# Windowed attention on Trainium2: softmax sums of four heads in one matmul, and value matmuls in alternating row tiles

## The chip, the cores and the metric

The kernel runs on one core of a Trainium2 chip. The metric is device time in microseconds (us), the median of several executions. All timed runs quoted here were fast, unless said otherwise. The granted clock, the mean share of full speed that the chip grants the tensor engine, was 0.998 or more in them, but for e11 (0.991 to 0.997) and the single run of e12 (0.993). Ratios are the mean time of one kernel's fast runs over the mean of the fast runs of the kernel before in the same rounds, so they are not quite the ratio of the medians quoted next to them. The kernel before takes about 510 us.

## The reference, cut to what matters

Two attention blocks share an input of 2048 rows of 1024; a gate mixes their outputs. The change touches block B only: each query attends to 8 keys, at distances 0, 2, ..., 14 behind it.

```python
H = 32; Dh = D // H                      # 32 heads of 32
W, dil = 8, 2
logits = einsum("bhsd,bhswd->bhsw", q, kg) * Dh ** -0.5
logits = where(mask, logits, -1e9)
attn = softmax(logits, axis=-1)
o = einsum("bhsw,bhswd->bhsd", attn, vg)
return o.transpose(...).reshape(B, S, D) @ wo
# ... and at the end: g * A(x) + (1 - g) * B(x)
```

The kernel sorts rows by parity, so a query's 8 keys are neighbours. A block of up to 57 queries then needs 64 keys, and a mask takes care of which.

## The kernel before

The program is a list of operations that a scheduler orders for each engine, with an estimated cost for each. Block B's attention is cut into 18 "fills". A fill is two halves (h) of up to 57 queries, for all 32 heads. It has three steps: the scores S on the tensor engine (64 small matmuls), exponential and mask, and then the "value burst": for each head and half one matmul of the values with the exponentials E, and one of a block of ones with E, which gives the softmax sums. ScalarE then takes exp(-ln(sum)) and VectorE multiplies.

```python
def s_fn(e):                                   # scores: 64 matmuls, 32 rows x 64 weight columns
    for c in range(8):
        for h in range(2):
            for j in range(4):
                last = e.matmul(SO[j]...[64 * h:64 * h + 64, :], kT[32 * j:32 * j + 32, ...], qT[...],
                                start=True, stop=True, tile_position=(32 * j, 64 * h))
    return last
P.op("pe", s_fn, 0.45, mode="r", ...)
# ... E = exp(scores), E *= mask
for g in range(2):                             # two groups of 16 heads
    def each(e, g=g):
        for o in range(2):                     # 0: values, 1: sums
            for c in range(4):
                for h in range(2):
                    for j in range(4):
                        hd = 16 * g + 4 * c + j
                        w = vt[64 * h:64 * h + 64, hd * 32:hd * 32 + 32] if o == 0 else ones[64 * h:64 * h + 64, :]
                        last = e.matmul(SO[2 * g + h].ap((4 * o + c) * nq, (4 * o + c + 1) * nq)[32 * j:32 * j + 32, :], w,
                                        E[64 * h:64 * h + 64, (8 * j + 4 * g + c) * nq:(8 * j + 4 * g + c + 1) * nq],
                                        start=True, stop=True, tile_position=(64 * h, 32 * j))
        return last
    P.op("pe", each, 0.35, mode="c", ..., name="PV")
    # ... ScalarE: L = Ln(sums); L = Exp(-L); VectorE: qT = values * L
```

A matmul here is a pair of instructions: a load of its weights (64 rows x 32 columns, into one of 8 tiles of the array: row tile h, column tile j), and the matmul that streams nq = 57 columns (56 in the last fills) through that tile. A value burst is 2 x (32 + 32) = 128 pairs. Between bursts the engine does dense 128x512 matmuls of the projections. I count the pairs of a burst from 0.

## Time and profile before

| | before |
|---|---|
| time | 510.26 us (509.35 to 511.56) |
| tensor engine (PE) busy | 99% of the span, granted clock 0.999 |
| VectorE / ScalarE busy | 52% / 39% |
| small pairs: 18 score bursts, 18 value bursts | 1152 and 2304 |

The page of the kernel before: busy time of each engine with its share and number of instructions, then the chain of work that ended last, by engine and by line. PEld is the weight-load side of the tensor engine, DVE is VectorE, ACT ScalarE, POOL GpSimd, SPq the queue of SyncE that issues transfers; "issue" is time in which the engine waited for nothing that the profile shows.

```profile
PE 501.5 (99%) x6121; PEld 239.4 (47%) x6121; DVE 265.0 (52%) x456; ACT 196.2 (39%) x335; POOL 6.6 (1%) x30
...
PE 96%; SPq 2%; DMA 1%; ACT 1%; issue 0%; DVE 0%
PE ps_all L1324 75%; PE ps_all L1674 11%; PE ps_all L1449 4%; PE ps_all L1427 2%; PE ps_all L1599 1%; SPq L1294 1%; DMA w_4_52<-in_B_wqkv_dram 1%; PE ps_all L1520 1%; PE ps_all L1577 1%; SPq L1299 0%; PE ps_all L1392 0%; ACT ra_50_98 L1601 
```

The tensor engine bounds the kernel, and the value bursts (line 1449) hold 4% of the chain, the scores (line 1427) 2%.

Groups of matmuls by shape, kernel before: line, engine, names, rows*columns of the tile, streamed operand, count, then busy us and mean ns of one.

```profile
L1427 PE MATMUL ps_all<-qT_50,kT_51 32*64 32x57 bf16 x1024 | 11.2, 200 | 0.0
L1449 PE MATMUL ps_all<-E_40_88,ones_58 64*32 64x57 bf16 x512 | 7.3, 195 | 0.0
...
L1449 PE MATMUL ps_all<-E_39_87,v_43_91 64*32 64x57 bf16 x192 | 2.4, 192 | 0.0
```

The 195 ns of one matmul say little: they overlap, and 512 of them take 7.3 us. What counts is the time from start to start. For that, here is one value burst in order of time on the weight-load side, kernel before (start us, length us, what):

```profile
144.38 0.19 PEld L1449 LDWEIGHTS ps_all<-E_40_88,v_44_92 64*32 64x32 bf16 x32 [0.42 <-DVE mx_54_102 L1280]
144.51 0.44 PEld L1449 LDWEIGHTS ps_all<-E_40_88,ones_58 64*32 64x32 bf16 x32
144.87 0.35 PEld L1449 LDWEIGHTS ps_all<-E_40_88,v_44_92 64*32 64x32 bf16 x32
145.16 0.35 PEld L1449 LDWEIGHTS ps_all<-E_40_88,ones_58 64*32 64x32 bf16 x32
145.55 0.55 PEld L1324 LDWEIGHTS ps_all<-xT_49,w_5_53 128*128 128x128 bf16 x4
```

From the first small load to the next dense one are 1.17 us for 128 pairs. (The releaser in brackets is merely the last event before: every burst that follows dense work starts 93 or 94 ns over a normal step in this trace, whatever is named.) The single starts in the trace give the anatomy. Dense matmuls start every 216 ns; the "cost" of a burst below is the time from the last dense matmul before it to the first after it, less those 216 ns:

```
value burst before, 128 pairs, cost 1262 ns (all six that stand alone: 1261 or 1262)
  last dense matmul to first small one     309 ns, so 93 over a normal step
  loads of pairs 0 to 31                   3 to 4 ns apart
  loads of pairs 32 and 33                 25 and 101 ns later; pair 33 is 229 ns after pair 0
  from there                               8 or 9 ns apart (8.33 on average), but one step of 34 ns at pair 96
  (by matmuls, as in the prediction: pair 32, the 33rd, starts 223 ns after pair 0)
  last load to the next dense load         128 ns
score burst, 64 pairs, cost 727 ns: the same quick 32 (loaded in 114 ns, those above in 104) and the same 8.33 ns
```

### The profile page before, as it was taken

Reading aid. Unit: us, or ns where it says so; the run is one execution under the profiler, and the core shown is the slowest. Engines: PE = TensorE matmul, PEld = TensorE weight load, DVE = VectorE, ACT = ScalarE, POOL = GpSimd, SP = SyncE. Lnnn points to the kernel's source line nnn. Section 1 sums busy time; section 2 is a strip of 40 time slices with the busy share of each in tenths; the row PEclk is TensorE's granted clock in tenths of the full one; section 3 lists DMA queues with packets and bytes.
Section 4 is the critical chain, followed back from the end, with each engine's and each line's share of the span. In section 5 each row is a group of like instructions: output and inputs, shape, how many; then the busy total and the mean of one; then the engine's idle time right before and its main releaser. Section 6 shows DMA issues by size and latency. Waiting matters only on the chain.

```text
span 507.9 us, 13377 instructions
## 1 busy us (share of the span) xinstructions
PE 501.5 (99%) x6121; PEld 239.4 (47%) x6121; DVE 265.0 (52%) x456; ACT 196.2 (39%) x335; POOL 6.6 (1%) x30
## 2 busy tenths in 40 slices
PE   8999999999999999999999999999999999999996
PEld 3444444444555555555555555544444444444443
DVE  3112245655667675554555555488776673334443
ACT  1111111111444454655565465479965453110000
POOL 5000000000000000000000000000000000000000
PEclk9999999999999999999999999999999999999999
DMA  8999980000033060100010100500000000002212
GB/s 227 198 209 320 352 248 1 1 0 1 24 104 109 23 199 24 35 25 23 23 35 23 35 3 4 168 0 0 1 1 1 1 1 0 3 29 76 83 74 76
DMA packets 47417, 35.04 MB, mean 69 GB/s; under 512 B 22261, under 2 KB 43125, under 8 KB 47354
## 3 DMA queue, kind: packets, MB, share of 16 engines
q1 hardware_dynamic: 46810, 33.59, 23.2%
q8 instruction: 50, 0.82, 0.7%
q10 hardware_dynamic: 544, 0.52, 0.3%
q14 instruction: 13, 0.11, 0.1%
HBM read 21.51 MB, written 8.40 MB: 59 GB/s over the span
## 4 chain that ended last, share of the span: by engine, by line
PE 96%; SPq 2%; DMA 1%; ACT 1%; issue 0%; DVE 0%
PE ps_all L1324 75%; PE ps_all L1674 11%; PE ps_all L1449 4%; PE ps_all L1427 2%; PE ps_all L1599 1%; SPq L1294 1%; DMA w_4_52<-in_B_wqkv_dram 1%; PE ps_all L1520 1%; PE ps_all L1577 1%; SPq L1299 0%; PE ps_all L1392 0%; ACT ra_50_98 L1601 0%; ACT ra_52_100 L1601 0%; ACT ra_51_99 L1601 0%; ACT e_27_75 L1333 0%
## 5 line engine op out<-in xcount | busy, mean ns | idle before, releaser
L1324 PE MATMUL ps_all<-xT_49,w_6_54 128*128 128x512 bf16 x512 | 118.1, 379 | 0.1
L1324 PE MATMUL ps_all<-w_4_52,xT_49 128*128 128x512 bf16 x512 | 116.0, 379 | 0.7 <-DMA xT_49<-in_A_x_dram 0.7
L1324 PEld LDWEIGHTS ps_all<-xT_49,w_6_54 128*128 128x128 bf16 x512 | 49.5, 98 | 59.2 <-ACT ra_52_100 L1601 0.6
L1324 PEld LDWEIGHTS ps_all<-w_4_52,xT_49 128*128 128x128 bf16 x512 | 48.3, 98 | 59.4 <-DMA xT_49<-in_A_x_dram 2.1
L1324 PE MATMUL ps_all<-w_7_55,xT_49 128*128 128x512 bf16 x256 | 59.3, 379 | 0.0
L1324 PE MATMUL ps_all<-xT_49,w_5_53 128*128 128x512 bf16 x256 | 58.4, 379 | 0.0
L1674 PE MATMUL ps_all<-w_7_55,qT_50 128*128 128x512 bf16 (+1 forms) x264 | 55.4, 373 | 0.0
L1324 PE MATMUL ps_all<-w_5_53,xT_49 128*128 128x512 bf16 x192 | 42.7, 379 | 0.0
L1674 PEld LDWEIGHTS ps_all<-w_7_55,qT_50 128*128 128x128 bf16 x264 | 25.8, 98 | 29.7
L1324 PEld LDWEIGHTS ps_all<-xT_49,w_5_53 128*128 128x128 bf16 x256 | 24.5, 98 | 29.2 <-issue 0.4
L1324 PEld LDWEIGHTS ps_all<-w_7_55,xT_49 128*128 128x128 bf16 x256 | 24.1, 98 | 28.0 <-issue 0.3
L1324 PEld LDWEIGHTS ps_all<-w_5_53,xT_49 128*128 128x128 bf16 x192 | 18.8, 98 | 22.6
L1359 ACT ACTIVATE qT_50<-ps_all 128x512 bf16<-128x512 f32 x15 | 9.0, 597 | 37.1 <-PE ps_all L1324 37.1
L1356 ACT ACTIVATE kT_51<-ps_all 128x512 bf16<-128x512 f32 x14 | 8.4, 597 | 35.5 <-PE ps_all L1324 35.5
L1358 DVE TENSOR_SCALAR xT_49<-ps_all,g_65 128x512 bf16<-128x512 f32 x15 | 11.2, 749 | 19.9 <-PE ps_all L1324 19.9
L1280 DVE TENSOR_TENSOR mx_54_102<-mx_54_102,kT_51 128x1024 bf16<-128x1024 bf16 x16 | 11.1, 691 | 16.9 <-ACT kT_51 L1356 16.9
L1280 DVE TENSOR_TENSOR mx_54_102<-mx_54_102,qT_50 128x1024 bf16<-128x1024 bf16 x16 | 11.1, 691 | 16.8 <-ACT qT_50 L1359 16.7
L1459 DVE TENSOR_TENSOR qT_50<-ps_all,L_41_89 128x456 bf16<-128x456 f32 (+1 forms) x18 | 11.3, 628 | 11.6 <-ACT L_41_89 L1458 11.6
L1355 DVE CAST kT_51<-ps_all 128x512 bf16<-128x512 f32 x18 | 12.3, 684 | 7.6 <-PE ps_all L1324 7.6
L1433 ACT ACTIVATE E_39_87<-ps_all 128x1824 bf16<-128x1824 f32 (+1 forms) x9 | 15.2, 1688 | 2.3 <-PE ps_all L1427 1.8
L1433 ACT ACTIVATE E_40_88<-ps_all 128x1824 bf16<-128x1824 f32 (+1 forms) x9 | 15.2, 1688 | 0.6
L1324 PE MATMUL ps_all<-w_5_53,pq_8_56 128*128 128x512 bf16 x64 | 15.1, 379 | 0.0
(179 smaller groups left out, 518.8 us busy)
## 6 DMA issues: line engine op xcount, KB each, us to landing
w_5_53<-in_B_wqkv_dram SPq DMA_DIRECT2D x2, 1024.0 KB, 7.8
w_6_54<-in_B_wqkv_dram SPq DMA_DIRECT2D x2, 1024.0 KB, 8.5
w_4_52<-in_A_wqkv_dram SPq DMA_DIRECT2D x2, 1024.0 KB, 9.3
w_7_55<-in_A_wqkv_dram SPq DMA_DIRECT2D x2, 1024.0 KB, 8.2
w_5_53<-in_A_wo_dram SPq DMA_DIRECT2D x2, 1024.0 KB, 5.6
w_6_54<-in_A_wqkv_dram SPq DMA_DIRECT2D x2, 1024.0 KB, 5.4
w_7_55<-in_B_wo_dram SPq DMA_DIRECT2D x2, 1024.0 KB, 5.9
out_dram<-o_60_108 SPq DMA_DIRECT2D x8, 256.0 KB, 2.0
```

Source lines behind the costliest of these rows:

```text
L1280: P.op("dve", lambda e, m=m, op=op: e.tensor_tensor(m[:, 0:n], m[:, 0:n], src, op), 0.08 + n / 1920.0, reads=[m.all(), reg], writes=[m.all()],
L1294: return P.op("sp", lambda e: e.dma_start_transpose(xT[:, :, t * 128:(t + 1) * 128], x2[e_, r * 128:(r + 1) * 128, :]), 1.5, writes=[xT.pa ...
L1324: last = e.matmul(bank.ap(), lhs(dc), rhs(dc), start=(dc == 0), stop=(dc == 7))
L1355: fd = lambda e: e.tensor_copy(dst, src())
L1356: fa = lambda e: e.activation(dst, src(), ACT.Copy)
L1358: fd = lambda e: e.tensor_scalar(dst, src(), scale, None, op0=ALU.mult)
L1359: fa = lambda e: e.activation(dst, src(), ACT.Copy, scale=scale)
L1427: last = e.matmul(SO[j].ap(c * nq, (c + 1) * nq)[64 * h:64 * h + 64, :], kT[32 * j:32 * j + 32, c, t0 + k0[h]:t0 + k0[h] + 64], qT[32 * j: ...
L1433: P.op("act", lambda e: e.activation(E[:, 0:32 * nq].rearrange("p (j q) -> p j q", j=4), ps[:, 4:8, 0:8 * nq], ACT.Exp), act(32 * nq), rea ...
L1449: last = e.matmul(SO[2 * g + h].ap((4 * o + c) * nq, (4 * o + c + 1) * nq)[32 * j:32 * j + 32, :], w, E[64 * h:64 * h + 64, (8 * j + 4 * g ...
L1459: P.op("dve", lambda e, L=L, pb=pb, g=g: e.tensor_tensor(qT[:, 4 * g:4 * g + 4, t0 + qs:t0 + qs + 2 * nq].rearrange("p c (h q) -> p h c q" ...
L1674: last = e.matmul(bank.ap(0, f1 - f0), qT[:, dc, t * 128:(t + 1) * 128], ws[3][:, dc, f0:f1], start=(dc == 0), stop=(dc == 7))
```

## The change: intent and diff

The sums of four heads c are neighbours in E, and the weights (ones) are the same, so one matmul of 4 x 57 = 228 columns can do the work of four. Each half of a burst then has 32 + 8 = 40 pairs, a burst 80 instead of 128. The values, besides, alternate between the two row tiles instead of doing four pairs in one and then four in the other. Two cost estimates for the scheduler change.

```diff
-P.op("pe", s_fn, 0.45, mode="r", ...)
+P.op("pe", s_fn, 0.55, mode="r", ...)
 ...
-for o in range(2):
-    for c in range(4):
-        for h in range(2):
-            for j in range(4):
-                ... one matmul of nq columns, weights vt or ones ...
+for c in range(4):
+    for j in range(4):
+        for h in range(2):
+            ... value matmul of nq columns into SO[2 * g + h].ap(c * nq, (c + 1) * nq)[32 * j:32 * j + 32, :] ...
+for j in range(4):
+    for h in range(2):
+        last = e.matmul(SO[2 * g + h].ap(4 * nq, 8 * nq)[32 * j:32 * j + 32, :], ones[64 * h:64 * h + 64, :],
+                        E[64 * h:64 * h + 64, (8 * j + 4 * g) * nq:(8 * j + 4 * g + 4) * nq],
+                        start=True, stop=True, tile_position=(64 * h, 32 * j))
-P.op("pe", each, 0.35, mode="c", ...)
+P.op("pe", each, 0.36, mode="c", ...)
```

More of the change, by code (lines that the diff above doesn't have):

```diff
@@ L1429, in s_fn @@
                 return last
-            P.op("pe", s_fn, 0.45, mode="r", reads=[kT.part((0, 8), (t0 + k0[0], t0 + k0[1] + 64)), qT.part((0, 8), (t0 + qs, t0 + qs + 2 * nq))],
+            P.op("pe", s_fn, 0.55, mode="r", reads=[kT.part((0, 8), (t0 + k0[0], t0 + k0[1] + 64)), qT.part((0, 8), (t0 + qs, t0 + qs + 2 * nq))],
                  writes=[s.iv for s in SO], name="S")
@@ L1442, in each @@
                     def each(e, g=g):
-                        for o in range(2):
-                            for c in range(4):
+                        for c in range(4):
+                            for j in range(4):
                                 for h in range(2):
-                                    for j in range(4):
-                                        hd = 16 * g + 4 * c + j
-                                        w = vt[64 * h:64 * h + 64, hd * 32:hd * 32 + 32] if o == 0 else ones[64 * h:64 * h + 64, :]
-                                        last = e.matmul(SO[2 * g + h].ap((4 * o + c) * nq, (4 * o + c + 1) * nq)[32 * j:32 * j + 32, :], w,
-                                                        E[64 * h:64 * h + 64, (8 * j + 4 * g + c) * nq:(8 * j + 4 * g + c + 1) * nq],
-                                                        start=True, stop=True, tile_position=(64 * h, 32 * j))
+                                    hd = 16 * g + 4 * c + j
+                                    e.matmul(SO[2 * g + h].ap(c * nq, (c + 1) * nq)[32 * j:32 * j + 32, :], vt[64 * h:64 * h + 64, hd * 32:hd * 32 + 32],
+                                             E[64 * h:64 * h + 64, (8 * j + 4 * g + c) * nq:(8 * j + 4 * g + c + 1) * nq],
+                                             start=True, stop=True, tile_position=(64 * h, 32 * j))
[3 more added lines that the diff above has]
+                                                E[64 * h:64 * h + 64, (8 * j + 4 * g) * nq:(8 * j + 4 * g + 4) * nq],
+                                                start=True, stop=True, tile_position=(64 * h, 32 * j))
                         return last
                     bi = [SO[2 * g].iv, SO[2 * g + 1].iv]
-                    P.op("pe", each, 0.35, mode="c", reads=[vt.all(), ones.all(), E.all()], writes=bi, name="PV")
+                    P.op("pe", each, 0.36, mode="c", reads=[vt.all(), ones.all(), E.all()], writes=bi, name="PV")
                     L, _ = Lr.next()
```

## The prediction

> **What bounds the kernel.** The tensor engine. The page's first part: PE 501.5 of 507.9 us (99%), VectorE 52%, ScalarE 39%; the granted clock is full throughout; the chain that ended last is 96% PE. Line 1449 (sums and values) is 4% of it, the scores (line 1427) 2%. PE time saved there is saved from the whole; nothing else can give much.
>
> **What one value burst costs.** There are 18. In order of time, dense 128x512 matmuls start every 216 ns. From the last one before a burst to the first after it are 1478 ns, so a burst costs 1262 ns, the same to 2 ns wherever no other small burst adjoins: 22.7 us in all. Inside, by starts:
> - 93 ns over a normal step before the first small matmul;
> - 32 matmuls 3 to 4 ns apart, then a pause of 97 ns; the 33rd starts 223 ns after the first;
> - then one pair (weight load, matmul) per 8.33 ns, 4.17 ns per instruction; one hiccup of some 26 ns;
> - 128 ns from the last start to the next dense matmul.
>
> Sum: 93 + 223 + 95 x 8.33 + 26 + 128 = 1261.
>
> The score burst (64 pairs, weights of 64 columns, already alternating between row tiles) keeps the same 8.33 ns after the same quick 32. [...]
>
> **What the change does.** Streamed columns stay the same. Per burst, 64 sums of 57 columns become 16 of 228: 80 pairs, not 128. The instruction order built from both kernels shows hardly anything else moved.
> - Removed: 48 x 8.33 = 400 ns.
> - Added: the last sum streams 171 columns more; [...].
> - [...]
> - Alternating row tiles: about 0, as the scores alternate and get the same pace.
>
> Expected burst: 93 + 223 + 47 x 8.33 + (0 to 30) + 199 = 905 to 935 ns, saving about 340. Times 18: 6.1 us, all on the chain. ScalarE and VectorE have slack; the scheduler's new costs shift a few bursts by eight matmuls: about 0.
>
> **Predicted: 504.2 us (-1.2%), 8 in 10 between 502.6 and 506.6.** Chances: faster by over 2% 0.02, within 2% 0.97, slower by over 2% 0.01.
>
> **What would show it right.** Bursts of about 0.92 us between dense matmuls, 8.33 ns steps in the values after the 32nd, about 200 ns from the last sum to the next dense matmul; dense matmuls and score bursts (727 ns) unchanged; PE 98 to 99% busy.
>
> **What would make it wrong.** (a) Two row tiles of the same columns cannot stream long matmuls at once: eight sums then take about 190 ns per half, the burst exceeds 1.0 us, the gain is 3 to 4 us. (b) [...] alternation then speeds up the values, and the gain exceeds 7 us. (c) The pause of 97 ns moves or repeats.

The sum is whole: 93 + 223 + 47 x 8.33 + (0 to 30) + 199 = 905 to 935 ns a burst, about 340 saved, 6.1 us for 18 bursts. The 199 is the 128 ns of the trace and 71 more, for the 171 columns that the last sum streams beyond 57. The 0 to 30 leaves room for the hiccup of 26 ns and for a wait of the next value behind the first half's sums, mostly hidden. At the dense pace of the trace, 512 columns in 216 ns, these times are, as estimates: 72 ns for 171 columns; 96 ns for a sum of 228, and so a wait of 29 beyond eight pairs at 8.33 ns; and 192 ns for two such sums one after the other, the "about 190" of (a).

## The result, and the profile after

The changed kernel took 504.05 us (503.54 to 504.76, 4 runs), the kernel before in the same rounds 509.85 us. The ratio is 0.9881, with a 95% interval of 0.9854 to 0.9909: 1.2% faster, inside the range and within 0.2 us of the number predicted. Run again later, it gave 504.56 us and 0.9880.

The page after, the same parts as before:

```profile
PE 488.5 (97%) x5190; PEld 232.6 (46%) x5257; DVE 264.6 (53%) x456; ACT 192.9 (38%) x335; POOL 6.6 (1%) x30
...
PE 95%; issue 2%; DMA 1%; ACT 1%; SPq 0%; DVE 0%
PE ps_all L1324 76%; PE ps_all L1677 11%; PE ps_all L1427 2%; PE ps_all L1447 2%; PE ps_all L1602 1%; PE ps_all L1452 1%; PE ps_all L1523 1%; DMA xT<-in_A_x_dram 1%; PE ps_all L1580 1%; ACT ra L1604 0%; PE ps_all L1392 0%; SPq L1294 0%; SPq
```

Weight loads fell from 6121 to 5257, by 864 = 18 x 48, as intended. The chain gives 3% to values and sums (lines 1447 and 1452) where it gave 4%. PE busy fell to 97% and "issue" appeared: that is no new idle time. The trace has 67 fewer matmuls than loads, and in the bursts I looked at the missing record is the first dense matmul after the burst; its load is there. The traces of e2 and e3 below, with 128 pairs and the time of the kernel before, also lack 67 records and also read 97%. I therefore measure the ends of bursts by loads.

Groups of matmuls by shape, after (values, sums, scores):

```profile
L1447 PE MATMUL ps_all<-E,v 64*32 64x57 bf16 x1024 | 12.4, 191 | 0.0
L1427 PE MATMUL ps_all<-qT,kT 32*64 32x57 bf16 x1024 | 11.3, 200 | 0.0
L1452 PE MATMUL ps_all<-E,ones 64*32 64x228 bf16 x256 | 10.4, 265 | 0.0
```

The value burst that answers to the one shown of before, weight-load side, after:

```profile
144.14 0.19 PEld L1447 LDWEIGHTS ps_all<-E,v 64*32 64x32 bf16 x32 [0.42 <-DVE mx L1280]
144.27 0.24 PEld L1452 LDWEIGHTS ps_all<-E,ones 64*32 64x32 bf16 x8
144.43 0.37 PEld L1447 LDWEIGHTS ps_all<-E,v 64*32 64x32 bf16 x32
144.75 0.15 PEld L1452 LDWEIGHTS ps_all<-E,ones 64*32 64x32 bf16 x8
145.00 0.98 PEld L1324 LDWEIGHTS ps_all<-xT,w 128*128 128x128 bf16 x6
```

From the first small load to the next dense one are now 0.86 us, 0.31 less. By single starts:

```
value burst after, 80 pairs, cost 960 ns (alone: 959 to 961)
  entry                                    93 over a normal step, as before
  pairs 0 to 31 quick; pair 33             231 ns after pair 0 (before: 229)
  from there                               8.33 ns, with steps of 22 and 21 ns at pairs 65 and 66 and of 34 ns at pair 72
  matmuls 40 and 41                        39 and 17 ns steps, then quick ones that catch up; matmul 40 starts 97 ns after 32,
                                           the sum in the same tile (228 columns: 96 ns at the dense pace, an estimate)
  last load to the next dense load         198 ns (before: 128)
score burst 728 ns
```

Adding up the costs of all small bursts of the trace (the few small matmuls of other parts included) gives 43.08 us before and 37.67 after, 5.41 less. The spans of the two profiled executions are 507.9 and 502.5 us, 5.4 less. So the gain is in the bursts. That the two agree so closely is luck: the span less its small bursts is 464.9 us in both, but 464.3 to 466.4 us over all the traces here without e11 and e12. The medians differ by 5.8 us; the remaining 0.4 us is inside the spread of single runs, which is over 1 us.

### The profile page after: what moved, and what is told of

Same layout as the page of the kernel before. It is cut to its first block, busy times and chain, and to the rows that moved or that the text cites. A ratio compares the mean times of both kernels' runs of the same rounds, so it can differ in the third digit from the quotient of the medians.

```text
span 502.5 us, 11582 instructions
## 1 busy us (share of the span) xinstructions
PE 488.5 (97%) x5190; PEld 232.6 (46%) x5257; DVE 264.6 (53%) x456; ACT 192.9 (38%) x335; POOL 6.6 (1%) x30
## 4 chain that ended last, share of the span: by engine, by line
PE 95%; issue 2%; DMA 1%; ACT 1%; SPq 0%; DVE 0%
PE ps_all L1324 76%; PE ps_all L1677 11%; PE ps_all L1427 2%; PE ps_all L1447 2%; PE ps_all L1602 1%; PE ps_all L1452 1%; PE ps_all L1523 1%; DMA xT<-in_A_x_dram 1%; PE ps_all L1580 1%; ACT ra L1604 0%; PE ps_all L1392 0%; SPq L1294 0%; SPq L1299 0%; ACT e L1333 0%; ACT ra L1605 0%
## 5 line engine op out<-in xcount | busy, mean ns | idle before, releaser
L1324 PE MATMUL ps_all<-w,xT 128*128 128x512 bf16 x922 | 207.8, 379 | 5.6 <-issue 4.0
L1324 PE MATMUL ps_all<-xT,w 128*128 128x512 bf16 x747 | 169.2, 379 | 2.5 <-issue 1.9
L1324 PEld LDWEIGHTS ps_all<-w,xT 128*128 128x128 bf16 x960 | 91.3, 98 | 110.3 <-issue 1.7
L1324 PEld LDWEIGHTS ps_all<-xT,w 128*128 128x128 bf16 x768 | 73.9, 98 | 88.8 <-ACT ra L1604 0.6
L1677 PE MATMUL ps_all<-w,qT 128*128 128x512 bf16 (+1 forms) x259 | 55.2, 373 | 0.3
L1677 PEld LDWEIGHTS ps_all<-w,qT 128*128 128x128 bf16 x264 | 25.8, 98 | 29.7
L1433 ACT ACTIVATE E<-ps_all 128x1824 bf16<-128x1824 f32 (+1 forms) x18 | 30.4, 1687 | 3.1 <-PE ps_all L1427 2.0
L1331 ACT ACTIVATE e<-ps_all 128x512 bf16<-128x512 f32 x32 | 19.1, 597 | 31.6 <-PE ps_all L1324 30.8
L1333 ACT ACTIVATE e<-ps_all 128x512 bf16<-128x512 f32 x32 | 19.2, 601 | 29.3 <-PE ps_all L1324 27.8
L1337 DVE SCALAR_TENSOR_TENSOR pk<-ps_all,e 128x512 bf16<-128x512 f32 x32 | 22.0, 688 | 0.8
L1604 ACT ACTIVATE ra<-ps_all,eps 128x512 f32<-128x512 f32 x32 | 21.5, 688 | 2.2 <-PE ps_all L1602 2.0
```

The lines of the kernel that those rows point to most:

```text
L1324: last = e.matmul(bank.ap(), lhs(dc), rhs(dc), start=(dc == 0), stop=(dc == 7))
L1331: P.op("act", lambda e: e.activation(e_[:, :], bank.ap(), ACT.Exp), act(512), reads=[bank.iv], writes=[e_.all()])
L1333: P.op("act", lambda e: e.activation(e_[:, :], bank.ap(), ACT.Exp, accum_out=qe[:, col:col + 1]), act(512) + 0.1, reads=[bank.iv], writes= ...
L1337: P.op("dve", lambda e: e.scalar_tensor_tensor(out=dst, in0=bank.ap(), scalar=0.0, in1=e_[:, :], op0=ALU.max, op1=ALU.add), dps(512), read ...
L1433: P.op("act", lambda e: e.activation(E[:, 0:32 * nq].rearrange("p (j q) -> p j q", j=4), ps[:, 4:8, 0:8 * nq], ACT.Exp), act(32 * nq), rea ...
L1604: P.op("act", lambda e: e.activation(R[:, :], db.ap(), ACT.Ln, bias=eps[:, :]), act(512), reads=[db.iv, eps.all()], writes=[R.all()])
```

## The experiments

The theory that entered them: a burst's pairs, behind the quick 32 and the pause, come at a fixed 8.33 ns per pair, whatever they stream, so pairs removed are what pays; long sums cost something at the end of the burst. Rivals: the alternation of row tiles pays; the scheduler's new order pays; or streamed columns set the time.

| run | pairs | burst alone, ns | all small bursts, us | median us (before beside it) | ratio (95%) |
|---|---|---|---|---|---|
| before | 128 | 1262 | 43.08 | | |
| the change, run again | 80 | 960 | 37.67 | 504.56 (511.08) | 0.9880 (0.9861 to 0.9899) |
| e1 merge only | 80 | 958 | 37.62 | 504.57 (510.09) | 0.9887 (0.9871 to 0.9903) |
| e2 alternation only | 128 | 1262 | 43.08 | 509.86 (510.09) | 0.9995 (0.9981 to 1.0010) |
| e3 costs only | 128 | 1262 | 43.08 | 509.86 (510.09) | 0.9990 (0.9977 to 1.0003) |
| e4 sums of two heads | 96 | 1018 | 38.69 | 505.17 (510.09) | 0.9899 (0.9883 to 0.9915) |
| e5 sums first | 80 | 934 | 37.21 | 503.61 (509.49) | 0.9883 (0.9867 to 0.9900) |
| e7 short sums (wrong result) | 80 | 861 | 35.89 | 502.65 (509.49) | 0.9861 (0.9843 to 0.9880) |
| e8 pairs put back | 128 | 1267 | 43.27 | 509.78 (509.49) | 1.0004 (0.9987 to 1.0020) |
| e9 sums of eight, first | 72 | 961 | 37.68 | 505.28 (509.49) | 0.9910 (0.9896 to 0.9924) |
| e10 late sums | 80 | 869 | 36.02 | 502.99 (511.08) | 0.9846 (0.9823 to 0.9868) |
| e11 sums of eight, in the middle | 72 | 822 | 40.04 | 513.49 (511.08) | 1.0047 (1.0027 to 1.0067) |
| e12 one signal | 80 | 934 | 41.51 | 514.45 (one run) | |

All runs passed the check of results, e7 too, though its sums are wrong by construction; so that check does not tell right sums from those of e7. No run has the number e6. In e11 and e12 the column of all small bursts holds the waits inside them.

### e1: the merge alone

The change without the alternation and with the old costs.

```diff
-for c in range(4):
-    for j in range(4):
-        for h in range(2):          # values, and the sums likewise
+for c in range(4):
+    for h in range(2):
+        for j in range(4):
```

> The sums of four heads are merged, but the values keep the order of the kernel before (four column tiles of one row tile, then the other), and the scheduler keeps its old costs. Theory ([...] 8.33 ns per pair of weight load and matmul): a value burst of 960 +- 15 ns as with the whole change, total within 0.15% of the whole change, about 0.988 of before. Rival (the alternation of row tiles gives a part of the gain): burst clearly above 975 ns and total above 0.990 of before.

Measured: 958 ns and 0.9887. The merge alone gives the whole gain.

### e2: the alternation alone

The kernel before with `for j` outside `for h`; sums stay at 57 columns.

> Only the order is changed: values and sums alternate between the two row tiles, the sums stay at 57 columns, 128 pairs. Theory: burst 1262 +- 10 ns, ratio to before 1.000 +- 0.002. Rival: burst shorter by 50 ns or more, ratio 0.998 or less.

One value burst of e2, weight-load side:

```profile
145.84 0.19 PEld L1449 LDWEIGHTS ps_all<-E,v 64*32 64x32 bf16 x32 [0.42 <-DVE mx L1280]
145.97 0.44 PEld L1449 LDWEIGHTS ps_all<-E,ones 64*32 64x32 bf16 x32
146.33 0.35 PEld L1449 LDWEIGHTS ps_all<-E,v 64*32 64x32 bf16 x32
146.62 0.35 PEld L1449 LDWEIGHTS ps_all<-E,ones 64*32 64x32 bf16 x32
147.00 0.55 PEld L1324 LDWEIGHTS ps_all<-xT,w 128*128 128x128 bf16 x4
```

The lengths are those of the kernel before, line for line. The burst costs 1262 ns, the ratio is 0.9995. Half of the change, by its title, does nothing. In this kernel four neighbouring pairs of one row tile and alternating ones go at the same 8.33 ns; in neither order do two neighbouring pairs use the same tile. At that pace a load in the kernel before starts 4 ns after the matmul ahead of it, in the same row tile too, where that matmul streams for some 24 ns (an estimate: 57 columns at 512 in 216 ns).

### e3: the scheduler's costs alone

The kernel before with 0.55 and 0.36 as the two costs.

> Only the scheduler's two costs are changed. Theory: the bursts stay at 1262 (values) and 727 ns (scores), only the number of dense matmuls between some bursts changes; ratio 1.000 +- 0.002. Rival (the new order is itself worth time): ratio 0.997 or less.

Measured: bursts of 1262 and 727 ns, ratio 0.9990. The interval allows 0.2%, so a tenth of a per cent from the order is not excluded; the summed bursts of 43.08 us show no part of the 5.4 us in it.

### e4: sums of two heads

The change with 16 sums of 114 columns per half instead of 8 of 228.

```diff
-for j in range(4):
-    for h in range(2):
-        ... ap(4 * nq, 8 * nq) ... E[..., (8 * j + 4 * g) * nq:(8 * j + 4 * g + 4) * nq]
+for d in range(2):
+    for j in range(4):
+        for h in range(2):
+            ... ap((4 + 2 * d) * nq, (6 + 2 * d) * nq) ... E[..., (8 * j + 4 * g + 2 * d) * nq:(8 * j + 4 * g + 2 * d + 2) * nq]
```

> The whole change, but sums of two heads in one matmul of 114 columns: 96 pairs, the same streamed columns. Theory: burst 1050 +- 25 ns (960 + 16 x 8.33 = 1093, less 48 ns because the last sum streams 114 columns fewer), exit from the last sum to the next dense matmul about 151 ns, total about 0.9915 of before. Rival (streamed columns set the burst): no difference from before or from the whole change.

Measured: 1018 ns, below the stated range; the exit was 150 ns as expected (the 48 ns are an estimate, 114 columns at the dense 512 in 216 ns). The steps at pairs 65 and 66 of the whole change are missing here. That is worth 27 ns (22 + 21 instead of 2 x 8.33 = 17, so 26 to 27), and 960 + 133 - 48 - 27 = 1018. So those steps belong to the long sums, and 114 columns are too short to cause them.

### e7: sums that stream only 57 columns

A wrong result: the first head's sum stands for all four.

```diff
-... ap(4 * nq, 8 * nq) ... E[..., (8 * j + 4 * g) * nq:(8 * j + 4 * g + 4) * nq]
+... ap(4 * nq, 5 * nq) ... E[..., (8 * j + 4 * g) * nq:(8 * j + 4 * g + 1) * nq]
-Ln reads the four sums
+Ln reads the one sum, broadcast
```

> Wrong result on purpose: as the whole change, with 16 sums of 57 columns instead of 228 (the sum of the first head stands for all four). 80 pairs, 36 percent of the streamed columns gone. Theory: burst 865 +- 10 ns: exit 128 instead of 198 ns, and the two steps of 22 and 21 ns in the second half's values (pairs 65 and 66) vanish, if they are the echo of the wait behind the long sums. If they stay, 890. Rival (streamed columns set the burst): burst below 750 ns.

```profile
144.12 0.19 PEld L1447 LDWEIGHTS ps_all<-E,v 64*32 64x32 bf16 x32 [0.42 <-DVE mx L1280]
144.24 0.24 PEld L1452 LDWEIGHTS ps_all<-E,ones 64*32 64x32 bf16 x8
144.40 0.35 PEld L1447 LDWEIGHTS ps_all<-E,v 64*32 64x32 bf16 x32
144.70 0.15 PEld L1452 LDWEIGHTS ps_all<-E,ones 64*32 64x32 bf16 x8
144.88 1.19 PEld L1324 LDWEIGHTS ps_all<-xT,w 128*128 128x128 bf16 x7
```

Measured: 861 ns, exit 127, no steps at 65 and 66. Three eighths of the streamed columns are gone (three quarters of the sums, which are half of all; the 36 percent of the expectation is a slip), yet the burst is only 99 ns shorter: 71 at the exit, 27 from the steps. Streamed columns do not set the pace.

### e8: the pairs put back

After each half's sums, 24 repeats of them on 8 columns only, which write the same values again.

```diff
+for _ in range(3):
+    for j in range(4):
+        for h in range(2):
+            last = e.matmul(SO[2 * g + h].ap(4 * nq, 4 * nq + 8)[32 * j:32 * j + 32, :], ones[64 * h:64 * h + 64, :],
+                            E[64 * h:64 * h + 64, (8 * j + 4 * g) * nq:(8 * j + 4 * g) * nq + 8], ...)
```

> The whole change and, after each half's sums, 24 repeated sums of only 8 columns, which write the same values again: 128 pairs as in the kernel before, with few more columns than after. Theory: the gain is given back: burst 1250 to 1290 ns, ratio to before 1.000 +- 0.003. Rival (streaming or weight columns matter): burst within 100 ns of the 960 of the change.

```profile
144.10 0.19 PEld L1447 LDWEIGHTS ps_all<-E,v 64*32 64x32 bf16 x32 [0.42 <-DVE mx L1280]
144.23 0.24 PEld L1452 LDWEIGHTS ps_all<-E,ones 64*32 64x32 bf16 x8
144.39 0.28 PEld L1458 LDWEIGHTS ps_all<-E,ones 64*32 64x32 bf16 x24
144.59 0.37 PEld L1447 LDWEIGHTS ps_all<-E,v 64*32 64x32 bf16 x32
144.91 0.15 PEld L1452 LDWEIGHTS ps_all<-E,ones 64*32 64x32 bf16 x8
144.97 0.28 PEld L1458 LDWEIGHTS ps_all<-E,ones 64*32 64x32 bf16 x24
145.27 1.19 PEld L1324 LDWEIGHTS ps_all<-xT,w 128*128 128x128 bf16 x7
```

Again 1.17 us from the first small load to the next dense one. The burst costs 1267 ns and the ratio is 1.0004: 48 nearly empty pairs per burst give the whole gain back. 960 + 48 x 8.33 - 92 (exit 106 instead of 198) = 1268. This settles the main cause: what is paid for is the pair, not what it streams, apart from the 99 ns that e7 showed the long sums to add.

### e5: sums first

The sums of each half ahead of its values.

> The whole change with the eight long sums of each half issued ahead of its values. Theory: the long stream of the last sum no longer delays the next dense matmul (exit 128 instead of 198 ns), and the wait of the first values for the first sums falls into the pause after the 32nd pair, so the burst is 890 +- 25 ns; total lower than the whole change by about 1.2 us (0.9855 of before). Rival (the exit is a fixed cost of the mode change and the wait moves to the front): burst 950 ns or more.

A miss: 934 ns instead of 890, above the stated range. The exit fell to 127, against 198 in the change, so the exit is no fixed cost, and the steps at 65 and 66 went, as expected (71 + 27 saved). But pair 33 came 301 ns after pair 0 instead of 229: the wait was not hidden in the pause, it pushed the pause back by 72 ns. 960 - 71 - 27 + 72 = 934. In time, 503.61 us and 0.9883 cannot be told from the change itself; the 0.46 us fewer in the bursts are too little for that.

### e9: sums of eight heads, first

One matmul of 456 columns per tile, ahead of all values; sums in two banks, values in the other two; one logarithm, exponential and product per fill.

```diff
+def sums(e):  ... SO[h].ap(0, 8 * nq) ... E[64 * h:64 * h + 64, 8 * j * nq:8 * (j + 1) * nq] ...        # 8 pairs
+def each(e):  ... SO[2 + h].ap(c * nq, (c + 1) * nq) ... for c in range(8) ...                          # 64 pairs
```

> Sums of eight heads in one matmul of 456 columns, ahead of all values, in two banks of their own; the values of all heads in the other two; one logarithm, one exponential and one product per fill instead of two. 72 pairs. Theory: eight sums occupy their tiles 190 ns, then 24 quick values, so the 33rd pair is at about 270 ns instead of 223, partly caught up; burst 93 + 223..270 + 39 x 8.33 + 128 = 770 to 820 ns; with 80 rather than 128 pairs already worth 5.4 us, this is 2.5 to 3.5 us more: total about 0.982 of before. Rival (long streams do not overlap across all eight tiles): burst above 900 ns.

A miss: 961 ns. (Its 190 ns are an estimate: 456 columns at 512 in 216 ns are 192.) Eight pairs fewer, and the burst is no shorter than that of the change. Pair 33 came 396 ns after pair 0. The expectation had named over 900 ns as the sign of its rival, that long streams do not overlap across tiles; the single starts exclude it, since the eight values behind the sums wait 180 ns once and then start 3 or 4 ns apart, so the eight tiles had streamed together. And the total, 505.28 us, is longer than the bursts explain: right after the last fill the tensor engine waits for the transposed key-value product (0.66 us in one place) where it does not in the change, since the scheduler made another order there; steps over 216 ns between dense loads add up to 6.1 us in this trace and 5.1 in that of the change.

The three values of pair 33 fit one pattern. The delay against short values is 301 - 229 = 72 ns for sums of 228 columns and 396 - 229 = 167 ns for 456. From the dense pace (512 columns in 216 ns) the additional streaming is, as an estimate, 171 x 216 / 512 = 72 and 399 x 216 / 512 = 168 ns. So the load of pair 33 comes later by what pair 0 streams longer. A burst that begins with short matmuls has 32 quick pairs at its head; with long sums first the loads stop earlier as well, at pair 16 (a step of 61 ns in e5, 157 ns in e9).

A second reading fits as well: the load of pair 33 comes 189 to 191 ns after the matmul of pair 8 starts, the next one in the tile of pair 0, in the change, e5 and e9 alike. Since a tile comes round every 8 pairs in all these bursts, no run here tells the two apart, and what holds the load is not shown.

Taken as a rule of thumb for all pairs of these bursts (the load of pair i+33 comes no earlier than about 229 ns after pair i, and later by what pair i streams beyond 57 columns), the first reading gives the odd steps too. At 8.33 ns a pair, 33 pairs are 275 ns. The 229 ns behind a short matmul hold nobody up. Behind a sum of 228 columns they are 301, 26 ns late: the sums begin at pair 32, and the steps are at 65. Behind a sum of 114 columns they would be about 253 (an estimate), and e4 has no steps. The step of 34 ns (26 more than 8) stands in every run so far 33 pairs behind the end of the first half's operation, the matmul that signals to ScalarE (it raises the semaphore on which ScalarE waits): 63 and 96 before, 39 and 72 after and in e5 and e7, 47 and 80 in e4, 63 and 96 in e8, 7 and 40 in e9. The next runs tested that.

### e12: one signal

The order of matmuls of the change, but both halves as one operation with one signal.

```diff
-for g in range(2): P.op("pe", each, 0.36, ...)      # two operations, two signals
+P.op("pe", each, 0.72, ...)                         # both halves in one
```

> The whole change in the same order of matmuls, but both halves in one operation of the program: one signal at the end of the burst instead of one after each half. Theory: the step of 34 ns at pair 72 (32 pairs behind the first signal) becomes 8, the steps of 22 and 21 ns at pairs 65 and 66 stay; burst 934 +- 6. Rival (the 34 ns belong to the start of the second sums): burst stays 960.

Measured: 934 ns, steps of 24 and 20 at pairs 65 and 66, none at 72. The burst is what was expected, 960 - 26 = 934. The total is another matter: 514.45 us in the one run, which is slower than the kernel before. With one signal at the end, ScalarE's work for the first half can only begin after the whole burst, the scheduler put the next scores eight dense matmuls later, and the last fill slid behind the end of its stage. The waits of the tensor engine in e12, longest first (us in total, times, longest):

```profile
...
PE ps_all L1447 <- DVE E L1436: 2.4, 1, 2.4
PE ps_all L1363 <- DVE warm L1272: 1.3, 1, 1.3
PE ps_all L1324 <- DVE w L1355: 1.1, 1, 1.1
PE ps_all L1324 <- DMA xT<-in_A_x_dram: 1.0, 2, 0.8
PE ps_all L1589 <- DVE kvT L1355: 0.9, 1, 0.9
PE ps_all L1427 <- DVE qT L1471: 0.8, 1, 0.8
```

and in the change, run beside it, where the list has no wait for VectorE but that for the first constant:

```profile
...
PE ps_all L1363 <- DVE warm L1272: 1.3, 1, 1.3
PE ps_all L1324 <- DMA xT<-in_A_x_dram: 0.7, 1, 0.7
```

One value burst waits 2.4 us for its exponentials, and the dense work behind it waits for the folded weights. Which part of the 10 us each of these waits costs is left open. The granted clock has a part in it too. The page's row of the granted clock (40 slices of the span, in tenths of full speed) has a 7, where that of the change has nines only:

```profile
PEclk9999999999999999999999999799999999999999
```

From 325.75 to 332.58 us of the span the trace grants half the clock, from within the wait of 2.4 us on; it alone accounts for the mean of 0.993. Eight dense matmuls behind that wait start 427 ns apart instead of 216, which is 1.7 us lost. (e11, below, has the same wait and 3.41 us at half clock.)

This stretch also tests the pace. The value burst that waited runs wholly at half clock (327.05 to 327.82 us), and still pairs 34 to 47 are loaded 8 or 9 ns apart, and so are the last 13. So far as this one burst shows, the pace of 8.33 ns does not follow the clock of the tensor engine; the waits in between did grow (pair 33 comes 257 ns after pair 0, not 230).

### e11: sums of eight heads, in the middle

As e9, but 40 values first, then the 8 long sums, then 24 values; the first signal after the sums.

> Sums of eight heads (456 columns) as in the earlier run of 72 pairs, but after 40 value pairs instead of ahead of all. [...] burst 93 + 223 + 8 x 8.33 + about 282 + 128 = 793, with 20 either way, because a long sum neither holds back the 33rd pair nor the exit. The built order puts the scores one group of eight later than the whole change, as in the earlier run, and so some 1 us may be lost after the last fill: total 0.983 to 0.985 of before. Rival: as in the earlier run, burst near 960.

The burst is near the expectation: 822 instead of 793. The tiles that stream 456 columns hold the next values up by 142 ns (the step ahead of the matmul behind the sums), not all of which is caught up, and the exit is 144. The total is a miss, 513.49 us and 1.0047, for the same reason as in e12, as far as its trace shows (the same wait of 2.4 us heads its list): the built order has the scores a group later and the last fill behind its stage, and the trace has a value burst that costs 3.9 us with its wait. A burst 138 ns shorter than that of the change, and a kernel 9 us slower.

### e10: late sums

The two signals stay, and the sums are moved to where nothing stands 33 pairs behind them: values of the first half (pairs 0 to 31), two of the four value rounds of the second half, the first half's sums (48 to 55, first signal), a value round, the second half's sums (64 to 71), the last value round.

```diff
+def first(e):   values g=0 c=0..3, values g=1 c=0, 1, sums g=0
+def second(e):  values g=1 c=2, sums g=1, values g=1 c=3
+P.op("pe", first, 0.44, ...); P.op("pe", second, 0.22, ...)
```

> The whole change with the sums moved: values of the first half (32 pairs), two of four value rounds of the second half (16), the sums of the first half, a value round, the sums of the second half, the last value round. The first signal to the other engines is raised after pair 56 instead of 40. Theory ([...] a long sum stays 71 ns longer): no long sum has a pair 32 behind it, so the two steps of 22 and 21 ns go; the signal has none 32 behind it either, so the step of 34 ns goes; a value round follows the last sums, so the exit is 128 ns. Burst 93 + 223 + 47 x 8.33 + 128 = 835, with 20 more at most; total 2.2 us below the whole change, about 0.984 of before. Rival (the steps belong to the place in the burst, or to the start of a group of sums): burst 880 or more.

One burst of e10, weight-load side:

```profile
144.43 0.43 PEld L1447 LDWEIGHTS ps_all<-E,v 64*32 64x32 bf16 x48 [0.42 <-DVE mx L1280]
144.78 0.15 PEld L1455 LDWEIGHTS ps_all<-E,ones 64*32 64x32 bf16 x8
144.85 0.15 PEld L1447 LDWEIGHTS ps_all<-E,v 64*32 64x32 bf16 x8
144.92 0.15 PEld L1455 LDWEIGHTS ps_all<-E,ones 64*32 64x32 bf16 x8
144.98 0.15 PEld L1447 LDWEIGHTS ps_all<-E,v 64*32 64x32 bf16 x8
145.20 1.84 PEld L1324 LDWEIGHTS ps_all<-xT,w 128*128 128x128 bf16 x10
```

All steps are gone: behind pair 33 every load comes 8 or 9 ns after the one before. The burst costs 869 ns, 34 more than expected where 20 were allowed, because the last eight values wait for the tiles of the last sums (a step of 43 ns) and nothing is left behind them to catch up: the exit is 159 ns, not 128. Against the change, 27 + 26 + 39 = 92 ns a burst are saved, by 18 is 1.66 us; the medians in the same rounds differ by 504.56 - 502.99 = 1.57 us, and the runs do not overlap (502.72 to 503.42 against 503.67 to 505.91). This version beats both kernels: 0.9846 of before.

### The change, run again

> The whole change again, beside the two reorderings on the same chip, so that they are compared with it in the same rounds: burst 960 ns, ratio to before 0.988 +- 0.0015.

Measured: 960 ns and 0.9880.

## Why the prediction was right

- **What bounds it.** Right. The gain in the profiled spans, 5.4 us, is the gain in the bursts, 5.41 us, to within the 2 us by which the rest of the span varies between traces.
- **Removed: 48 pairs of 8.33 ns.** Right, and now shown: e8 gives 48 pairs back without their columns and the gain goes; e7 takes three eighths of the burst's columns away and gains 99 ns of 960.
- **Added at the end: 71 ns.** Right: the exit is 198 against a stated 199; with short sums (e7) it is 127.
- **Alternation: about 0.** Right: e2 is 0.9995 with an unchanged burst; e1, without it, has the whole gain.
- **Scheduler's costs: about 0.** As far as e3 can tell, right (0.9990, interval to 1.0003).
- **The wait behind the first sums, "0 to 30" with the hiccup.** This term was mis-sized. The matmuls do catch up at once (steps down to 2 ns behind pair 41), but 33 pairs behind the long sums the loads stop for 27 ns. With the 26 ns behind the first signal, which the sum allowed as part of 0 to 30, that is 53 ns over the even pace. The burst is 960 ns, not 905 to 935, and the gain in the bursts 5.4 us, not 6.1.
- **The final number** was 0.15 us off, by luck: two errors nearly cancelled. The gain was put at 6.1 us where the bursts account for 5.4 and the medians differ by 5.8; and it was taken off 510.26 us, where the same rounds gave 509.85 for the kernel before.
- **PE "98 to 99% busy"** was wrong on the page (97%), for a reason in the records: the matmul behind a burst is missing in the trace after.
- Of the three things named that could make it wrong, (a) did not happen: two row tiles stream long sums at once, since the value behind the first eight sums started 39 ns after the last of them; had the two row tiles streamed one after the other, 190 ns by the estimate beside the prediction, less the 67 (8 x 8.33) in which the sums are loaded, it would have waited over 120. (b), a gain from the alternation, is excluded by e1 and e2. (c) the pause moved only where long sums come first (e5, e9).

What sets the pace of 8.33 ns a pair is not shown. The runs show that it depends neither on streamed columns (8 in e8, 57), nor on weight columns (32 in values, 64 in scores), nor on the order of tiles (e2), nor, in the one burst of e12 at half clock, on the clock granted to the tensor engine.

## What to carry to other kernels

Where small tiled matmuls come in bursts, count instruction pairs, not columns, as long as the streams are short (8 and 57 columns here): merging matmuls with the same weights paid by the pair (8.33 ns), and reordering between tiles paid nothing (e2, 0.9995). Long streams are not free: sums of 456 columns at the head of a burst (e9) lost what eight fewer pairs had saved. Put them where nothing stands 33 pairs behind them and some short ones come after them, away from the head and the end of a burst (e10: 869 ns instead of 960). And judge a shorter burst by the whole kernel: merging operations to save a signal made the burst 26 ns shorter and the kernel 10 us slower in its one run (e12; e11, with six, lost 9), where other engines started later, the scheduler moved a stage's last work over its edge, and the wait was followed by a stretch at half clock (6.83 us in e12, 3.41 in e11).
